# Attention and a gated MLP on one core: which PSUM banks the joined attention-times-V blocks sum into

## The chip, the cores and the metric

The kernel runs on 1 core of one Trainium2 chip. The metric is the time of one execution on the device in microseconds; the time shown for a kernel is the median of its runs. The engines are TensorE (matmul; in the profile PE, its weight loads PEld), VectorE (DVE), ScalarE (ACT), GpSimd (POOL) and SyncE (SP, which here only issues DMAs).

## The reference

One transformer layer in parallel form: the same normalized input goes through sliding-window attention (A) and through a gated MLP (B), and both are added to the input.

```python
S, D, H, Dh, W, F = 2048, 576, 32, 18, 256, 4608      # bf16 inputs, batch 1
def _A_ref(x, wqkv, wo):
    q, k, v = ...                                     # x @ wqkv, split in 32 heads of 18
    scores = jnp.einsum("bhqd,bhkd->bhqk", q, k) * (Dh ** -0.5)
    mask = (idx[:, None] - idx[None, :] >= 0) & (idx[:, None] - idx[None, :] < W)
    p = _softmax(jnp.where(mask[None, None], scores, -1e9), axis=-1)
    o = jnp.einsum("bhqk,bhkd->bhqd", p, v)
    return o.transpose(0, 2, 1, 3).reshape(B, S, D) @ wo
def _B_ref(x, w1, w3, w2):
    h = _silu(x @ w1) * (x @ w3)
    return h @ w2
xn = _layernorm(x)
return x + _A_ref(xn, A_wqkv, A_wo) + _B_ref(xn, B_w1, B_w3, B_w2)
```

## The kernel before

**Order of work.** `add` (from L55) records every operation with the tiles that it reads and writes; `resolve` works out the semaphores that each needs, and each engine then runs its own operations in the order of recording. So the order in the file is the order on each engine, and a tile that is still being read or written by another engine becomes a wait.

The 2048 rows are worked on in NC = 4 chunks of 512 rows. A chunk has three stages:

- Projections of Q, K and V (`proj_begin`, `proj_part`, L502), in chunks 1 to 3; those of chunk 0 come ahead of the loop.
- The W1/W3 stage: 36 units, `for u in range(NF)`. A unit makes 128 of the 4608 columns of h. `unit_pairs` (L767) is called for nine steps n = 0 to 8, each a matmul of 64 rows of the array for W3 and one for W1, side by side, into two banks of 512 columns. Then `unit_tanh` (L776, ScalarE) reads the W1 bank, and `unit_h` issues two products on VectorE: `gs` (L782, from the tanh and the W1 bank) and `hT` (L785, from `gs` and the W3 bank). When the second has ended, both banks are free.
- The W2 stage: `p2_list` makes a list of items and `p2_item` issues them (`p2_mm`, L838). Output rows go in four groups of 128 (`tt`), in two halves of 288 columns, so there are four accumulators in each half, kept in `ACC[half]`. Items `w2` are steps over h, items `wo` and `wr` steps over the attention's output in `oT`; `wr` is what is left over of it. `q` is a pair of accumulators: q = 0 is `ACC[half][0:2]`, q = 1 is `ACC[half][2:4]`. In `rest()` there is one `wr` item for each pair; in half 0 both come first, ahead of the nine W2 tiles (`fc`) of sixteen `w2` items each. Items other than those for the whole 128 rows are two matmuls of 64 rows of the array.

**Attention inside the W1/W3 stage.** `score_step` puts one step of scores between matmul steps of a unit: `scores` (L632) writes the two scores' banks `SC`, `exps` (L641, ScalarE) reads them and writes probabilities into a slot, `masks` (L669, POOL) multiplies the slot by the mask. Slots lie in `pt`, and in memory lent by others: `stage`, `hT`, from unit 30 `uq`, `ofin` and `od`, from unit 32 a weight buffer (shown as `w`). Heads are in eight groups; two groups make a pair j = 0 to 3, whose attention-times-V (`pv`, L697) sums into two banks. `BLOCKS` says which pairs are done together: in chunk 0 pairs 0 and 1 alone and (2, 3) joined; in chunks 1 to 3 (0, 1) and (2, 3). A joined block is issued by `pv_block(u, True)` in the middle of a unit, at the (u, n) of `AT`: block (0, 1) at (16, 2), (16, 3) and (16, 5) in chunks 1, 2 and 3, block (2, 3) at (35, 1), (35, 3), (35, 4) and (35, 5) in chunks 0 to 3. `HOLD` = 10 keeps scores steps away in the ten matmul steps before it, and `nxt, soon` keep them away for 17 steps after.

**PSUM.** Of the eight banks two are `SC`, the other six are three pairs in a ring:

```python
        JOBS, SC = ((0, 1), (2, 3), (4, 5)), (6, 7)
        def job():
            nonlocal job_ctr
            i = job_ctr % 3
            job_ctr += 1
            return JOBS[i]
```

Every unit and every projection takes the next pair. In the loop over units, `b0 = jobs[u] = job()` comes ahead of the unit's steps, so a block in the middle of unit u takes what follows unit u's pair. `ACC` for the W2 stage consists of the pairs of units 34 and 35, the ring pair of the last block, and `SC`.

**Output of a block.** `pv_out` (L714, VectorE) transposes one bank into a float32 tile: the first into `uq`, the second into the memory of `ofin`, the third and fourth into two `pt` slots that `borrow` lends. `o_recip` (L718, VectorE) takes the reciprocals of the sums, `o_scale` (L723, POOL) scales one group into `oq`, `o_turn` (L730, VectorE, two halves) turns it back into `od`, and `o_pack` (L755) sends a pair from `od` to `oT` by DMA from SP. `later(u, what)` puts work off to just after `unit_h(u)`; what is put off beyond unit 35 is issued after the sixth item of the W2 stage.

Of the kernel before, what the change touches and what calls it, by code (L numbers as in the profile page):

```python
# [44 lines left out]
class _Prog:  # L45
# [13 lines left out]
    def add(self, eng, fn, r=(), w=(), j=(), dma=None, after=()):  # L59
        deps = []  # L60
        for k in r:
            deps += self.bufs[k].writers
        for k in w:
            g = self.bufs.get(k)
            if g is not None:
                deps += g.ahead(eng)
        for k in j:
            g = self.bufs[k].before
            if g is not None:
                deps += g.ahead(eng)  # L70
        op = _Op(eng, fn, deps + list(after), dma)
        op.after = tuple(after)
        self.n[eng] += 1
        op.pos = self.n[eng]
        if dma is not None:
            self.dma_count[dma] = self.dma_count.get(dma, 0) + 16
            op.cnt = self.dma_count[dma]
        for k in r:
            self.bufs[k].readers.append(op)
        for k in w:  # L80
            self.bufs[k] = _Gen([op], self.bufs.get(k))
        for k in j:
            self.bufs[k].writers.append(op)
        for k in w:
            if self.bufs[k].before is not None:
                self.bufs[k].before.before = None
        self.ops.append(op)
        return op
# [76 lines left out]
def bass_parallel_sum__sliding_block__glu_gated_swiglu__prompt_kernel(  # L165
# [21 lines left out]
    NF = F // 128  # L187
# [3 lines left out]
    scale = float(Dh) ** -0.5  # L191
# [6 lines left out]
    with ExitStack() as es:  # L198
# [80 lines left out]
        JOBS, SC = ((0, 1), (2, 3), (4, 5)), (6, 7)  # L279
        ACC = [[], []]  # L280
        job_ctr = 2
# [6 lines that stand above are left out]
# [418 lines left out]
        def borrow(slots):  # L706

            for i, n in enumerate(slots):
                uqs[2 + i:3 + i] = [pt[:, n, :, :].rearrange("p r q -> p (r q)").bitcast(dt.float32)]
                uq_keys[2 + i:3 + i] = [[("pt", n)]]  # L710

        def pv_out(b, i):
            to = uqs[i]
            add("dve", lambda e: e.transpose(to, PS[:, b, :]), r=[("ps", b)], w=uq_keys[i])  # L714

        def o_recip(i):
            u3 = uqs[i].rearrange("p (n d) -> p n d", d=32)
            add("dve", lambda e: e.reciprocal(rden[i][:], u3[:, :, Dh]), r=uq_keys[i], w=[("rden", i)])  # L718

        def o_scale(i):  # L720
            u3 = uqs[i].rearrange("p (n d) -> p n d", d=32)
            o3 = oq[:, :].rearrange("p (n d) -> p n d", d=32)[:, :, 0:Dh]
            add("pool", lambda e: e.tensor_tensor(  # L723
                o3, u3[:, :, 0:Dh], rden[i][:].unsqueeze(2).to_broadcast([128, CH // 32, Dh]), ALU.mult),
                r=uq_keys[i] + [("rden", i), "oq0"], w=["oq"])

        def o_turn(g, half):
            i = g // 2 % NOD
            c0 = half * (CH // 2)
            add("dve", lambda e: e.transpose(od[i][:, g % 2, c0:c0 + CH // 2], oq[:, c0:c0 + CH // 2]),  # L730
                r=["oq", "oq0"], **{"j" if half or g % 2 else "w": [("od", i)]})
# [58 lines left out]
        def p2_list(c):  # L790

            seq = []
            for half in range(2):
                sw = half

                def phases(items):
                    nonlocal sw
                    for turn in (sw, 1 - sw):
                        for q in range(2):
                            yield from ((q, turn, it) for it in items)  # L800
                    sw = 1 - sw

                def rest():
                    return [("wr", half, 0, q, 0, 0) for q in range(2)]

                whole = half == 1 and c + 1 == NC
                if half == 0:
                    seq += rest()
                for fc in range(NFC - whole):
                    tile = [("w2", half, fl, q, turn, fc) for q, turn, fl in phases(range(4))]  # L810
                    seq += tile + [("next", half, 0, 0, 0, fc)]
                if whole:
                    seq.append(("keep", half, 0, TB - 1, 0, 0))
                    for tt in range(TB):
                        for turn in (None,) if tt < TB - 1 else (-2, -1):
                            seq += [("w2", half, fl, tt, turn, NFC - 1) for fl in range(4)]
                            seq += [("wo", half, kd, tt, turn, 0) for kd in range(5)]
                            seq += [("out", half, 0, tt, turn, 0)]
                    continue
                seq += [("wo", half, kd, q, turn, 0) for q, turn, kd in phases(range(2))]  # L820
                two = [("wo", half, kd, q, turn, 0) for q, turn, kd in phases(range(2, 4))]
                ends = rest() if half == 1 else []
                seq += two[:4]
                for q in range(2):
                    seq += two[4 + 2 * q:6 + 2 * q] + (ends[q:q + 1] if half == 1 else [])
                    seq += [("out", half, 0, 2 * q + r, 0, 0) for r in range(2)]
            return seq
# [210 lines left out]
        main, rest = span_main, span_last  # L1038
# [5 lines left out]
        for c in range(NC):  # L1044
# [23 lines left out]
            jobs = {}  # L1068
# [3 lines left out]
            def later(u, what):  # L1072
                side.setdefault(u, []).append(what)
# [29 lines left out]
            def pv_block(u, mid=False):  # L1103
                nonlocal next_pv, clock, free, job_ctr, nxt, soon
                block = BLOCKS[c][next_pv]
                assert u > turned.get(c, -1) + 1, (c, u, turned)
                next_pv += 1
                ends = next_pv == len(BLOCKS[c])
                pairs = [job(), SC] if ends else [job() for _ in block]
                for j, banks in zip(block, pairs):  # L1110
                    pv(c, j, banks)
                clock += PV_COST[c] * len(block)
                if len(block) == 2:
                    nxt, soon = max(nxt, clock + 17), max(soon, clock + 17)
                groups = range(2 * block[0], 2 * block[-1] + 2)
                was = [pt_of[(c, g, s)] for g in groups for s in range(NS)]
                assert all(NF - 2 * NHP + 2 * n > u for kind, n in was if kind == "h"), (c, u)
                was = [sl for sl in was if sl[0] != "h"]
                lent = [n for kind, n in was if kind == "pt"][-2:] if len(block) == 2 else []
                free += [sl for sl in was if sl not in [("pt", n) for n in lent]] + [("pt", n) for n in lent]  # L1120

                def drain(pairs=pairs, lent=lent):
                    borrow(lent)
                    for i in range(2 * len(pairs)):
                        pv_out(pairs[i // 2][i % 2], i)
                    for i in range(2 * len(pairs)):
                        o_recip(i)
                    o_scale(0)

                drain() if mid else later(u, drain)  # L1130
                if ends:
                    job_ctr -= 1
                    ACC[:] = [[*jobs[NF - 2], *pairs[0]], [*SC, *jobs[NF - 1]]]
                else:
                    job_ctr += mid
                k = 0
                for i, g in enumerate(groups):
                    for half in range(2):
                        k += 1 if (i, half) not in ((0, 1), (2, 1)) else 0
                        later(u + k, lambda g=g, half=half: o_turn(g, half))  # L1140
                    if i + 1 < len(groups):
                        later(u + k, lambda i=i: o_scale(i + 1))
                turned[c] = u + k
                for i, j in enumerate(block):
                    later(u + (4 + 3 * i if len(block) == 2 else 5), lambda j=j: o_pack(j, "sp"))
                    for n in range(4, 12, 2 if c else 1) if j == 0 else ():
                        later(u + n // 2 + 3 if c else u + n + 1,
                              lambda n=n: o_pack(0, "sp", n, n + 2) if c else o_pack(0, "act", n, n + 1))
# [19 lines left out]
            for u in range(NF):  # L1168
# [50 lines left out]
                if c == 0 and u == 18:  # L1219
                    rows = A_wo[0:4 * Dh, :].rearrange("(n d) f -> n d f", d=Dh)  # L1220
                    add("sp", lambda e: e.dma_start(wo[126:128, 0:4, :], rows[:, 0:2, :].rearrange("n d f -> d n f")),
                        j=["wo"], dma="wo")
                    for p in range(2):
                        add("sp", lambda e, p=p: e.dma_start(wo[64 * p:64 * p + 64, 4, :], rows[:, 2:Dh, :]),
                            j=["wo"], dma="wo")
# [11 lines left out]
            banks = ()  # L1237
# [52 lines left out]
```

## Time and profile before

| | us |
|---|---|
| median of 3 runs | 558.56 (558.46 to 558.62) |
| the profiled execution | 558.54 |
| its span in the trace | 556.8 |
| mean granted TensorE clock | 1.00 |

The lines of the profile stand in the prediction. Groups read: line, engine, operation, out<-in by tile names, shapes, count | busy us, mean ns of one | idle time of the engine just before them, and what ended it. Lines of the timeline read: start (us), duration (us), engine, line, operation, out<-in, how many were merged [idle before, and what ended it]. A duration of several merged matmuls runs from the start of the first to the end of the last; ends of matmuls are modelled. Lines of the list of waits read: who waited <- for whom: total us, how often, the longest. Chunk 0's W1/W3 stage ends near 101 us of the span, those of chunks 1, 2 and 3 near 239, 377 and 514 us; each time the W2 stage follows for some 40 us.

### The profile page before, as it was taken

How to read it: one execution, taken by the hardware profiler on the slowest of the kernel's cores; microseconds unless marked ns; L12 is line 12 of the kernel's file. 1: busy time of each engine (PE TensorE's matmuls, PEld its weight loads, DVE VectorE, ACT ScalarE, POOL GpSimd, SP SyncE). 2: the span in 40 equal slices, each digit the busy share in tenths (PEclk: the TensorE clock that was granted, in tenths of full speed). 3: DMA queues.
4: the chain of work that ended last, by engine and by line, in shares of the span. 5: the costliest groups of instructions: out<-in, count | busy, mean ns of one | idle time of the engine just before them, and what ended most of it. 6: DMA issues, size and time to landing. Idle time of an engine off the chain costs nothing.

```text
span 556.8 us, 18354 instructions
## 1 busy us (share of the span) xinstructions
PE 551.2 (99%) x8071; PEld 365.6 (66%) x8071; DVE 313.2 (56%) x587; ACT 259.3 (47%) x365; POOL 211.2 (38%) x380
## 2 busy tenths in 40 slices
PE   8999999999999999999999999999999999999998
PEld 5555544777688644477768854557887665445787
DVE  8466797710478886651057978655105567866311
ACT  7457776000387568600047757760005774875000
POOL 4424675400056565530005755643000553663100
PEclk9999999999999999999999999999999999999999
DMA  9997899587567853756646985476673673641750
GB/s 249 204 199 174 197 209 213 133 201 184 134 141 165 164 136 102 171 144 193 186 106 139 177 151 137 106 167 162 176 184 87 138 171 101 151 116 44 192 152 23
DMA packets 128038, 86.00 MB, mean 154 GB/s; under 512 B 35702, under 2 KB 125646, under 8 KB 127958
## 3 DMA queue, kind: packets, MB, share of 16 engines
q1 hardware_dynamic: 89138, 62.80, 50.3%
q10 hardware_dynamic: 38820, 22.02, 15.7%
q8 instruction: 63, 1.03, 0.8%
q14 instruction: 17, 0.14, 0.1%
HBM read 71.29 MB, written 2.36 MB: 132 GB/s over the span
## 4 chain that ended last, share of the span: by engine, by line
PE 96%; DVE 1%; ACT 1%; issue 1%; DMA 0%; ACTq 0%
PE ps L767 50%; PE ps L838 29%; PE ps L502 9%; PE ps L632 5%; PE ps L697 3%; DMA xp<-in_A_x_dram 0%; DVE gs L782 0%; DVE hT L785 0%; ACT th L776 0%; ACTq L567 0%; ACT stage L515 0%; DVE stats L398 0%; ACT hT L392 0%; DVE uq L714 0%; PE ps L431 0%
## 5 line engine op out<-in xcount | busy, mean ns | idle before, releaser
L767 PE MATMUL ps<-xnT,w 64*128 64x512 bf16 x1400 | 190.1, 376 | 0.0
L767 PE MATMUL ps<-xnS,w 64*128 64x512 bf16 x1120 | 156.9, 376 | 0.0
L838 PE MATMUL ps<-w,hT 64*128 64x288 bf16 x2292 | 143.5, 282 | 0.0
L782 DVE SCALAR_TENSOR_TENSOR gs<-th,ps 128x512 bf16<-128x512 bf16 x144 | 97.9, 680 | 79.7 <-ACT th L776 79.1
L838 PEld LDWEIGHTS ps<-w,hT 64*128 64x128 bf16 x2292 | 115.3, 94 | 26.0 <-issue 0.2
L767 PEld LDWEIGHTS ps<-xnT,w 64*128 64x128 bf16 x1400 | 80.3, 94 | 52.8 <-issue 0.6
L776 ACT ACTIVATE th<-ps 128x512 bf16<-128x512 f32 x144 | 85.6, 594 | 61.3 <-PE ps L767 60.1
L785 DVE SCALAR_TENSOR_TENSOR hT<-gs,ps 128x512 bf16<-128x512 bf16 x144 | 98.9, 687 | 5.0
L669 POOL TENSOR_TENSOR pt<-pt,mk 128x256 bf16<-128x256 bf16 (+1 forms) x143 | 85.7, 625 | 26.7 <-ACT pt L641 26.7
L641 ACT ACTIVATE pt<-ps 128x1024 bf16<-128x1024 f32 (+1 forms) x80 | 80.8, 1010 | 27.0 <-PE ps L632 26.5
L767 PEld LDWEIGHTS ps<-xnS,w 64*128 64x128 bf16 x1120 | 64.2, 94 | 42.9 <-issue 0.6
L669 POOL TENSOR_TENSOR hT<-hT,mk 128x256 bf16<-128x256 bf16 (+1 forms) x52 | 30.4, 605 | 161.5 <-ACT hT L641 161.5
L515 ACT ACTIVATE stage<-ps 128x512 bf16<-128x512 f32 x16 | 9.6, 597 | 139.6 <-PE ps L502 137.3
L869 DVE TENSOR_TENSOR ofin<-ps,xp 128x288 bf16<-128x288 f32 x31 | 12.2, 451 | 99.2 <-PE ps L838 99.2
L632 PE MATMUL ps<-qv,kv 64*128 64x320 bf16 (+4 forms) x528 | 56.0, 260 | 0.0
L632 PEld LDWEIGHTS ps<-qv,kv 64*128 64x128 bf16 x528 | 30.3, 94 | 23.9 <-ACT uq L641 1.1
L502 PE MATMUL ps<-xnT,wp 64*128 64x512 bf16 (+1 forms) x360 | 39.3, 355 | 0.0
L730 DVE STREAM_TRANSPOSE od<-oq 128x256 bf16<-128x256 bf16 x64 | 25.4, 425 | 12.2 <-POOL oq L723 12.2
L641 ACT ACTIVATE hT<-ps 128x1024 bf16<-128x1024 f32 (+1 forms) x28 | 28.4, 1015 | 7.8 <-PE ps L632 7.6
L669 POOL TENSOR_TENSOR stage<-stage,mk 128x256 bf16<-128x256 bf16 (+1 forms) x44 | 24.9, 587 | 12.6 <-ACT stage L641 12.6
L502 PEld LDWEIGHTS ps<-xnT,wp 64*128 64x128 bf16 x360 | 21.4, 94 | 12.0 <-ACT va L551 0.2
L641 ACT ACTIVATE stage<-ps 128x1024 bf16<-128x1024 f32 (+1 forms) x24 | 24.3, 1014 | 6.1 <-PE ps L632 6.0
(92 smaller groups left out, 403.6 us busy)
## 6 DMA issues: line engine op xcount, KB each, us to landing
w<-in_B_w_dram SPq DMA_DIRECT2D x210, 192.0 KB, 4.2
w<-in_B_w_dram ACTq DMA_DIRECT2D x70, 288.0 KB, 3.5
xp<-in_A_x_dram SPq DMA_DIRECT2D x29, 144.0 KB, 4.2
out_dram<-ofin SPq DMA_DIRECT2D x31, 72.0 KB, 1.7
xnS<-xnT SPq DMA_DIRECT2D x8, 256.0 KB, 4.7
oT<-od SPq DMA_DIRECT2D x56, 36.0 KB
pt<-in_A_wqkv_dram SPq DMA_DIRECT2D x4, 288.0 KB, 5.4
hT<-in_B_w_dram SPq DMA_DIRECT2D x6, 192.0 KB, 7.3
```

Source lines behind the costliest of these rows:

```text
L502: op = add("pe", lambda e, out_=out_, st=st, mv=mv, n=n, r0=r0, first=first: e.matmul(out_, st, mv, start=first, stop=(part == 1 and n == ...
L632: add("pe", lambda e, r0=r0, out_=out_, kb=kb, q0=q0, nb=nb: e.matmul(out_, kb4[r0:r0 + 64, g, kb + NV - NB, :] if kb < 0 else kv[r0:r0 + ...
L641: add("act", lambda e: e.activation(pt_slot(sl)[:, :, 0:w], PS[:, SC[0]:SC[1] + 1, 0:w], ACT.Exp, scale=scale), r=[("ps", b) for b in SC], ...
L669: add("pool", lambda e, vb=vb, mm=mm: e.tensor_tensor(vb, vb, mm, ALU.mult), r=(key if n == 0 else []) + ["mk"], **{"w" if n == 0 else "j" ...
L697: add("pe", lambda e, p=p, q=q, pr=pr, sl=sl, g=g, pos=pos, q0=q0, nb=nb, col=col, first=first, n=n: e.matmul(PS[32 * q:32 * q + VW, banks ...
L730: add("dve", lambda e: e.transpose(od[i][:, g % 2, c0:c0 + CH // 2], oq[:, c0:c0 + CH // 2]), r=["oq", "oq0"], **{"j" if half or g % 2 els ...
L767: op = add("pe", lambda e, n=n, r0=r0, r=r, k=k, src=src: e.matmul(PS[:, b0 + r, :], wt[r0:r0 + 64, k, fl * 128:(fl + 1) * 128], src, star ...
L776: add("act", lambda e: e.activation(th[i][:], PS[:, bg, :], ACT.Tanh, scale=0.5), r=[("ps", bg)], w=[("th", i)])
L782: add("dve", lambda e: e.scalar_tensor_tensor(out=gs[i][:], in0=th[i][:], scalar=1.0, in1=PS[:, bg, :], op0=ALU.add, op1=ALU.mult), r=[("t ...
L785: add("dve", lambda e: e.scalar_tensor_tensor(out=hT[:, u, :], in0=gs[i][:], scalar=0.5, in1=PS[:, bu, :], op0=ALU.mult, op1=ALU.mult), r= ...
L838: op = add("pe", lambda e: e.matmul(PS[:, bank, 0:w], stat, move, start=new, stop=False, skip_group_check=True, **tile), r=keys, after=hel ...
L869: add("dve", lambda e: e.tensor_tensor(ofin[:, o, :], PS[:, bank, 0:HD], xp[xs[n]][:, d0:d0 + HD], ALU.add), r=[("ps", bank), ("xp", xs[n] ...
```

## The change

Five things are changed in two functions:

1. In a joined block the first pair of heads sums into `SC`, and the second into the ring's next pair, in every such block. Before, block (0, 1) took two ring pairs, and block (2, 3) one ring pair for pair 2 and `SC` for pair 3.
2. Block (0, 1) no longer advances the ring by one extra place (`job_ctr += mid` is gone).
3. Where block (2, 3) is drained, the ring pair, now that of pair 3, is still transposed first: the order of pairs is turned round there (`order`), and with it the order of scaling, turning and packing.
4. In block (0, 1) of chunks 1 to 3 only the first two transposes are issued at once; the other two, the reciprocals and the first scaling come after the products of the unit that the block stands in.
5. In half 0 of the W2 stage, four `w2` items of the first pair of accumulators come between the two `wr` items.

```diff
@@ p2_list
-                if half == 0:
-                    seq += rest()
                 for fc in range(NFC - whole):
                     tile = [("w2", half, fl, q, turn, fc) for q, turn, fl in phases(range(4))]
+                    if fc == half == 0:
+                        tile = [*rest()[:1], *tile[:4], *rest()[1:], *tile[4:]]
                     seq += tile + [("next", half, 0, 0, 0, fc)]
@@ pv_block
-                pairs = [job(), SC] if ends else [job() for _ in block]
+                pairs = [SC, job()] if len(block) == 2 else [job()]
                 for j, banks in zip(block, pairs):
                     pv(c, j, banks)
...
-                groups = range(2 * block[0], 2 * block[-1] + 2)
+                order = list(zip(block, pairs))[::-1 if ends else 1]
+                groups = [2 * j + i for j, _ in order for i in range(2)]
+                banks = [b for _, two in order for b in two]
...
-                def drain(pairs=pairs, lent=lent):
+                def drain(part=range(len(banks))):
                     borrow(lent)
-                    for i in range(2 * len(pairs)):
-                        pv_out(pairs[i // 2][i % 2], i)
-                    for i in range(2 * len(pairs)):
+                    for i in part:
+                        pv_out(banks[i], i)
+
+                def scale():
+                    for i in range(len(banks)):
                         o_recip(i)
                     o_scale(0)
 
-                drain() if mid else later(u, drain)
                 if ends:
+                    drain()
+                    scale()
                     job_ctr -= 1
-                    ACC[:] = [[*jobs[NF - 2], *pairs[0]], [*SC, *jobs[NF - 1]]]
+                    ACC[:] = [[*jobs[NF - 2], *pairs[1]], [*SC, *jobs[NF - 1]]]
+                elif mid:
+                    drain(range(2))
+                    later(u, lambda: drain(range(2, 4)))
+                    later(u, scale)
                 else:
-                    job_ctr += mid
+                    later(u, drain)
+                    later(u, scale)
...
-                for i, j in enumerate(block):
+                for i, (j, _) in enumerate(order):
                     later(u + (4 + 3 * i if len(block) == 2 else 5), lambda j=j: o_pack(j, "sp"))
```

## The prediction

> **What bounds the kernel now.** I read the page first, then the list of waits, then the timeline around the seven joined attention-times-V blocks and the starts of the W2 stage. The page and the waits:
>
> ```profile
> PE 551.2 (99%) x8071; PEld 365.6 (66%) x8071; DVE 313.2 (56%) x587; ACT 259.3 (47%) x365; POOL 211.2 (38%) x380
> PE 96%; DVE 1%; ACT 1%; issue 1%; DMA 0%; ACTq 0%
> PE ps L697 <- DVE hT L785: 1.0, 4, 0.3
> PEld ps L838 <- DVE ofin L714: 0.6, 2, 0.4
> DVE od L730 <- POOL oq L723: 12.2, 12, 1.9
> ```
>
> TensorE is busy for 99% of the span and holds 96% of the chain that ended last. No matmul is added or removed, so the change can only shorten or lengthen TensorE's waits. The waits name two places that it touches: the joined blocks (L697), held by the products of an earlier unit (L785), and the W2 stage (L838), held by the transposes (L714). An idle figure of modelled matmuls hides part of a stall, so I price each by the distance between matmul starts, against the same place where nothing is waited for.
>
> **The block at unit 16.** Old order: pair j = 0 takes the ring's next banks (those of unit 14), pair 1 the ones after (those of unit 15). Chunks 1, 2 and 3, in this order:
>
> ```profile
> 189.70 0.81 PE L767 MATMUL ps<-xnT,w 64*128 64x512 bf16 x6
> 190.02 0.69 DVE L785 SCALAR_TENSOR_TENSOR hT<-gs,ps 128x512 bf16<-128x512 bf16 x1
> 190.76 0.31 PE L697 MATMUL ps<-hT,va 64*20 64x320 bf16 x4 [0.24 <-DVE hT L785]
> 191.48 0.69 DVE L785 SCALAR_TENSOR_TENSOR hT<-gs,ps 128x512 bf16<-128x512 bf16 x1
> 191.78 0.30 PE L697 MATMUL ps<-hT,va 64*20 64x192 bf16 x8
> 192.31 0.31 PE L697 MATMUL ps<-pt,va 64*20 64x320 bf16 x4 [0.23 <-DVE hT L785]
> 327.86 1.04 PE L767 MATMUL ps<-xnT,w 64*128 64x512 bf16 x8
> 329.14 0.31 PE L697 MATMUL ps<-hT,va 64*20 64x320 bf16 x4 [0.24 <-DVE hT L785]
> 330.16 0.30 PE L697 MATMUL ps<-hT,va 64*20 64x192 bf16 x8
> 330.55 0.31 PE L697 MATMUL ps<-pt,va 64*20 64x320 bf16 x4
> 466.50 0.38 PE L767 MATMUL ps<-xnS,w 64*128 64x512 bf16 x2
> 466.81 0.31 PE L697 MATMUL ps<-hT,va 64*20 64x320 bf16 x4
> 467.82 0.30 PE L697 MATMUL ps<-hT,va 64*20 64x192 bf16 x8
> 468.02 0.31 PE L697 MATMUL ps<-pt,va 64*20 64x320 bf16 x4
> ```
>
> Two matmuls make a step; 0.216 us separate steps (row 194.86 below: five in 1.24 us, the last of them lasting 0.376). Chunk 3 waits for nothing: 0.31 us from the unit's last step to the block, 0.20 from the last wave of pair 0 to pair 1. In chunk 1 the last step starts at 189.70 + 2 x 0.216 = 190.13, the block at 190.76, 0.05 after the product of 190.02 ends: 0.63, so 0.32 too much. Pair 1 starts 0.53 after 191.78, 0.14 after the product of 191.48 ends: 0.33 too much. Chunk 2: 328.51 to 329.14 is 0.63 (0.32 too much), 330.16 to 330.55 is 0.39 (0.19 too much). Chunk 3 has nothing to give.
>
> With the change pair 0 goes to the scores' banks. Their last scores were written at least ten steps before (HOLD; 2.16 us), which leaves the exponentials time to read them out. Pair 1 takes unit 14's banks, free when the old pair 0 started. All four delays go: **0.32 + 0.33 + 0.32 + 0.19 = 1.16 us**. At worst none goes, if the scores' banks were busy as long.
>
> **What the changed ring costs.** The old code skipped one place after the block; now it doesn't. Counting on: unit 17 takes unit 15's pair (free before the block ended), unit 18 the pair of unit 16, unit 19 that of pair 1. Unit 18 has only unit 17's nine steps behind which unit 16's tanh and two products can pass. No scores step fills in: the next is due 17 steps after the block, in unit 18. Chunk 1:
>
> ```profile
> 193.66 1.31 DVE L714 STREAM_TRANSPOSE pt<-ps 128x512 f32<-128x512 f32 x2 [0.24 <-PE ps L697]
> 194.86 1.24 PE L767 MATMUL ps<-xnT,w 64*128 64x512 bf16 x10
> 195.15 0.30 DVE L718 RECIPROCAL rden<-pt 128x16 f32<-128x16 f32 x2
> 195.28 0.60 ACT L776 ACTIVATE th<-ps 128x512 bf16<-128x512 f32 x1 [4.56 <-PE ps L767]
> 195.91 0.69 DVE L782 SCALAR_TENSOR_TENSOR gs<-th,ps 128x512 bf16<-128x512 bf16 x1 [0.46 <-ACT th L776]
> 196.63 0.69 DVE L785 SCALAR_TENSOR_TENSOR hT<-gs,ps 128x512 bf16<-128x512 bf16 x1
> 196.80 0.59 PE L767 MATMUL ps<-xnT,w 64*128 64x512 bf16 x4
> ```
>
> The row of 194.86 begins with unit 16's last step, that of 196.80 with unit 17's. Unit 18 would start at 196.80 + 0.216 = 197.02. Unit 16's second product ends at 196.63 + 0.69 = 197.32; TensorE restarts after a single DVE signal in 0.06 (row 514.42 below, behind a transpose that ends at 514.36). So 197.38: **0.36 us late**. The distance is the same wherever the block stands in unit 16, since all of it lies after that unit's last step, so three chunks cost **1.08 us**; no row shows this wait itself. Behind the waiting matmul stands all of TensorE (unit 18, its scores step), and behind those ScalarE's tanh and exponential, so the whole stage moves by that much. Bounds: 0 if the pair is free after all, 3 x 0.44 = 1.32 with the slowest restart above (0.14). I take 0.06, the nearest in kind, since no tiling changes there.
>
> A rule of the Trainium skill speaks against this part: Perfetto Trace Analysis, section Optimizing Tensor Performance, Matmuls, asks that independent groups rotate through PSUM banks so that the evacuation of one overlaps the next group's matmuls. By that rule the old skip kept two units before a reuse and the new ring keeps one; taken alone that is rival E. The trace agrees as far as 2.46 us of evacuation (194.86 to 197.32) outlast 2.16 us of steps, but it has waits on the other side too.
>
> **VectorE's order.** Transposes 2 and 3 (1.31 us, row 193.66), four reciprocals (to 195.45, 0.48) and the first scaling move behind unit 16's products. Queued behind them are unit 17's products: chain free at 197.32 + 1.79 = 199.11, unit 17's products end at 200.52. Unit 20 needs them, at 197.38 + 2 x 1.94 = 201.26 at the earliest (scores steps push it on). Unit 19 needs transpose 3, at 198.6, and starts no sooner than 199.3. Both covered: cost 0. Without that cover each microsecond of lag beyond 0.7 costs one.
>
> **The block at unit 35.** Old: pair 2 on unit 33's banks, pair 3 on the scores' banks. Chunks 1, 2, 3:
>
> ```profile
> 234.26 1.03 PE L767 MATMUL ps<-xnT,w 64*128 64x512 bf16 x8
> 235.62 0.52 PE L697 MATMUL ps<-pt,va 64*20 64x320 bf16 x31 [0.33 <-DVE hT L785]
> 372.29 1.24 PE L767 MATMUL ps<-xnT,w 64*128 64x512 bf16 x10
> 373.65 0.52 PE L697 MATMUL ps<-pt,va 64*20 64x320 bf16 x31
> 510.41 0.38 PE L767 MATMUL ps<-xnS,w 64*128 64x512 bf16 x2
> 510.72 0.52 PE L697 MATMUL ps<-pt,va 64*20 64x320 bf16 x32
> ```
>
> Last step to block: 235.62 - 234.91 = 0.71, 373.65 - 373.15 = 0.50, 0.31. The third is the undisturbed figure again, so 0.40 and 0.19 are waits for unit 33, and go when pair 2 starts in the scores' banks: **0.59 us**. Chunk 0's block I leave at 0, which errs against the change if it waits at all.
>
> **The start of W2.** The banks of the block's ring pair receive the second `wr` group, after transposes 0 and 1. Chunks 1, 2, 3:
>
> ```profile
> 239.43 39.69 PE ps L838 x648
> 239.27 0.41 PE L838 MATMUL ps<-wo,oT 64*128 64x288 bf16 x4
> 377.08 0.57 PE L838 MATMUL ps<-wo,oT 64*128 64x288 bf16 x4
> 513.05 0.72 DVE L714 STREAM_TRANSPOSE uq<-ps 128x512 f32<-128x512 f32 x1 [1.19 <-PE ps L697]
> 513.69 0.67 DVE L714 STREAM_TRANSPOSE ofin<-ps 128x512 f32<-128x512 f32 x1
> 513.93 0.78 PE L838 MATMUL ps<-wo,oT 64*128 64x288 bf16 x4
> 514.42 0.09 PEld L838 LDWEIGHTS ps<-wo,oT 64*128 64x128 bf16 x1 [0.39 <-DVE ofin L714]
> ```
>
> Four matmuls take 0.41 us undisturbed; 0.16 and 0.37 more are waits. Now the ring pair is summed last, but the first transpose already started only when the whole block had ended (513.05): its target `uq` held probabilities of pair 3. So it moves by nothing. Four W2 steps go ahead of the second `wr`, each of two matmuls and so of 39.69 us / 648 x 2 = 0.12 us (first row, a piece of the chain of waits), 0.49 together, more than 0.37. They use unit 34's banks and products, ready long before. Gain: **0.53 us**; if the steps found something of their own to wait for, 0. The pack DMAs of pairs 3 and 2 change places on SP; the flush comes after the same six items, and the output projection that reads them runs nine W2 tiles (over 17 us) later: 0.
>
> **Sum.** 1.16 + 0.59 + 0.53 - 1.08 = 1.20 us saved. The profiled execution took 558.54 us (span 556.8); 558.54 - 1.20 = 557.34, and the median of the runs is 558.56, so **557.35 us**, 0.22% faster. What a measurement here can tell from no change is about 0.2%, 1.12 us: the forecast lies just past that line, at 557.44.
>
> **Rivals.**
>
> *B, the new wait takes most of it.* Unit 18 stalls longer than the rows say, 0.44 plus one refill of about 0.2 us (the distance between pairs in chunk 3), 0.64 x 3 = 1.92: 558.54 - 2.28 + 1.92 = **558.2**. For it: no row shows that wait. Against: the same restart in W2 took 0.06 and the old waits were priced in whole starts. Or the W2 gain fails: 557.9.
>
> *C, VectorE's lag becomes the bound (slower).* The place is the turn of the scaled output (L730), which stands in VectorE's queue between unit 17's and unit 18's products and waits for POOL's scaling, itself in line with the masks:
>
> ```profile
> L730 DVE STREAM_TRANSPOSE od<-oq 128x256 bf16<-128x256 bf16 x64 | 25.4, 425 | 12.2 <-POOL oq L723 12.2
> ```
>
> After two turns of this mean (0.85 us) unit 18's products run from 201.4 to 202.8; unit 21 wants the banks at 197.38 + 3 x 1.94 = 203.2. Beyond 0.4 us of waiting there, all goes to TensorE. The longest such wait listed is 1.9 us: 3 x 1.5 = 4.5, 557.35 + 4.5 = **561.9**. Against: the scaling needs only the first reciprocal, and unit 17's products give it 1.4 us.
>
> *D, unit 18's pair is free (the ring isn't what I counted).* Then 558.54 - 2.28 = **556.3**. Against: the deleted skip.
>
> *E, the old delays stay and only the new wait counts (slower).* If the 0.63 and 0.5 us at the blocks are the price of starting a block and not of waiting, only the lost distance between units is left: 558.54 + 1.08 = **559.6**. Against: the undisturbed 0.31 and 0.20 of chunk 3. The rule of the Trainium skill quoted above (Perfetto Trace Analysis, Matmuls) would give this case.
>
> **Chances.** Forecast 0.65, with its own range 557.0 to 557.8, of which 0.45 lies below 557.44; B 0.18; C 0.07; D 0.07; E 0.03. Faster 0.45 + 0.07 = 0.52, same 0.20 + 0.18 = 0.38, slower 0.07 + 0.03 = 0.10. The range 556.9 to 558.3 holds the forecast and B, and leaves out C, D and E.
>
> **What would show it.** In the profile after: no wait of L697 on L785 at the blocks of chunks 1 to 3, 0.31 us from last step to block and 0.20 between pairs; a new wait of L767 on L785 at the start of unit 18 three times, 0.2 to 0.3 us of modelled idle; no wait of L838 on L714. Wrong: a longer or second stall in units 18 to 21, a wait of the block for the exponentials, or a W2 start that waits for `hT` or `w`.

## The result, and the profile after

| | before | changed |
|---|---|---|
| median, us | 558.62 (558.44 to 560.62, 11 runs) | 557.11 (556.89 to 558.14, 11 runs) |
| ratio of the times | | 0.9971, 95% interval 0.9962 to 0.9981 |
| the profiled execution, us | 558.54 | 558.14 |
| its span, us | 556.8 | 556.4 |
| start of the long piece of W1/W3 matmuls in chunk 0 (120 in the chain of waits) | 21.04 | 22.11 |
| from there to the end of the span | 535.76 | 534.29 |

The change saves 1.51 us, 0.29% with an interval of 0.19% to 0.38%. The forecast was 557.35 us and 0.22%.

The profiled execution of the changed kernel is the slowest of its eleven: one of its first loads of x came about a microsecond later (the third statistics row on VectorE, L398, waits 1.20 us for it and starts at 6.80 us instead of 5.74), which moves everything behind it. That belongs to this execution and not to the program: in e9 below, the same program again, the long piece starts at 21.05. So below I compare traces from the start of chunk 0's W1/W3 matmuls on (the last row, here called the body). By the body the change saves 1.47 us, close to the medians.

The page and the list of waits after:

```profile
PE 551.5 (99%) x8071; PEld 362.1 (65%) x8071; DVE 312.6 (56%) x587; ACT 259.6 (47%) x365; POOL 211.2 (38%) x380
PE 98%; DVE 1%; ACT 1%; issue 0%
DVE od L730 <- POOL oq L723: 12.2, 12, 1.9
PEld ps L767 <- DVE hT L785: 1.7, 3, 0.7
PE ps L767 <- DVE hT L785: 0.4, 2, 0.2
```

The waits of the joined blocks (L697) on unit products (L785) and of W2 (L838) on transposes (L714) are gone from the list. In their place the units (L767) wait for the products of an earlier unit, three times. VectorE's wait for POOL's scaling (L730) is what it was, to the digit.

The block at unit 16, timeline of the changed kernel, chunks 1, 2 and 3:

```profile
190.72 0.81 PE L767 MATMUL ps<-xnT,w 64*128 64x512 bf16 x6
191.46 0.31 PE L697 MATMUL ps<-hT,va 64*20 64x320 bf16 x4
192.48 0.30 PE L697 MATMUL ps<-hT,va 64*20 64x192 bf16 x8
192.56 0.32 PE L697 MATMUL ps<-pt,va 64*20 64x320 bf16 x4
328.05 1.04 PE L767 MATMUL ps<-xnT,w 64*128 64x512 bf16 x8
329.02 0.31 PE L697 MATMUL ps<-hT,va 64*20 64x320 bf16 x4
330.04 0.30 PE L697 MATMUL ps<-hT,va 64*20 64x192 bf16 x8
330.22 0.31 PE L697 MATMUL ps<-pt,va 64*20 64x320 bf16 x4
466.20 0.38 PE L767 MATMUL ps<-xnS,w 64*128 64x512 bf16 x2
466.51 0.31 PE L697 MATMUL ps<-hT,va 64*20 64x320 bf16 x4
467.53 0.30 PE L697 MATMUL ps<-hT,va 64*20 64x192 bf16 x8
467.62 0.32 PE L697 MATMUL ps<-pt,va 64*20 64x320 bf16 x4
```

From the unit's last step to the block it is now 0.31 us (191.46 - 191.15), 0.32 and 0.31; before, 0.63, 0.63 and 0.31. From the last wave of the first pair to the second pair it is 0.08, 0.18 and 0.09; before, 0.53, 0.39 and 0.20. The block lost 1.40 us of waiting.

Two units further on, chunks 1, 2 and 3. Each first row begins with unit 16's last step, the second is its second product; the third holds the first matmuls of unit 18 (in chunk 1 behind unit 17's last step):

```profile
195.11 1.24 PE L767 MATMUL ps<-xnT,w 64*128 64x512 bf16 x10
196.88 0.69 DVE L785 SCALAR_TENSOR_TENSOR hT<-gs,ps 128x512 bf16<-128x512 bf16 x1
197.22 0.79 PE L767 MATMUL ps<-xnT,w 64*128 64x512 bf16 x4
332.55 1.24 PE L767 MATMUL ps<-xnT,w 64*128 64x512 bf16 x10
334.32 0.69 DVE L785 SCALAR_TENSOR_TENSOR hT<-gs,ps 128x512 bf16<-128x512 bf16 x1
335.07 0.61 PE L767 MATMUL ps<-xnT,w 64*128 64x512 bf16 x4 [0.20 <-DVE hT L785]
469.52 1.24 PE L767 MATMUL ps<-xnT,w 64*128 64x512 bf16 x10
471.29 0.69 DVE L785 SCALAR_TENSOR_TENSOR hT<-gs,ps 128x512 bf16<-128x512 bf16 x1
472.04 1.04 PE L767 MATMUL ps<-xnT,w 64*128 64x512 bf16 x8 [0.20 <-DVE hT L785]
```

Without a wait unit 18 starts ten steps of 0.216 us after unit 16's last: 334.71 in chunk 2, 471.68 in chunk 3. It starts at 335.07 and 472.04, 0.06 us after the product's end: 0.36 us late each time. In chunk 1 the two steps of the third row are 0.79 - 0.38 = 0.41 apart, so unit 18 starts at 197.63 instead of 197.27. Together 1.08 us. The listed 0.20 of idle is only the part that shows between modelled matmul ends.

The block at unit 35 in chunks 1 and 2, then the start of W2 in chunk 3:

```profile
234.88 1.03 PE L767 MATMUL ps<-xnT,w 64*128 64x512 bf16 x8
235.84 0.52 PE L697 MATMUL ps<-pt,va 64*20 64x320 bf16 x32
372.33 1.24 PE L767 MATMUL ps<-xnT,w 64*128 64x512 bf16 x10
373.50 0.52 PE L697 MATMUL ps<-pt,va 64*20 64x320 bf16 x32
513.03 0.82 PE L767 MATMUL ps<-xnS,w 64*128 64x512 bf16 x6
513.13 0.72 DVE L714 STREAM_TRANSPOSE uq<-ps 128x512 f32<-128x512 f32 x1 [1.30 <-PE ps L697]
513.77 0.67 DVE L714 STREAM_TRANSPOSE ofin<-ps 128x512 f32<-128x512 f32 x1
514.02 0.65 PE L838 MATMUL ps<-w,hT 64*128 64x288 bf16 x8
514.51 0.29 PE L838 MATMUL ps<-wo,oT 64*128 64x288 bf16 x2
```

The blocks start 0.31 us after the last step (235.84 - 235.53, 373.50 - 373.19); before, 0.71 and 0.50. In W2 the second `wr` item starts at 514.51, right behind the four `w2` items (514.02 + 4 x 0.1225). The second transpose ends at 514.44, 0.07 us before. That is hardly more than the 0.06 us that TensorE took to restart behind such a transpose in the kernel before, so it only just makes it. Before, the first transpose began with the next unit step (513.05 against 513.06); now it begins 0.10 us after it.

### The profile page after: what moved, and what is told of

It reads as the page before. It is cut to its first block, busy times and chain, and to the rows that moved or that the text cites. A ratio compares the mean times of both kernels' runs of the same rounds, so it can differ in the third digit from the quotient of the medians.

```text
span 556.4 us, 18354 instructions
## 1 busy us (share of the span) xinstructions
PE 551.5 (99%) x8071; PEld 362.1 (65%) x8071; DVE 312.6 (56%) x587; ACT 259.6 (47%) x365; POOL 211.2 (38%) x380
## 4 chain that ended last, share of the span: by engine, by line
PE 98%; DVE 1%; ACT 1%; issue 0%
PE ps L767 50%; PE ps L838 29%; PE ps L502 9%; PE ps L632 5%; PE ps L697 3%; PE ps L908 1%; DVE gs L782 0%; DVE hT L785 0%; ACT th L776 0%; ACT xnT L444 0%; PE ps L431 0%; DVE xn L416 0%; ACT xnT L450 0%; DVE stats L398 0%; ACT sd L371 0%
## 5 line engine op out<-in xcount | busy, mean ns | idle before, releaser
L767 PE MATMUL ps<-xnT,w 64*128 64x512 bf16 x1400 | 190.6, 376 | 0.4 <-DVE hT L785 0.4
L767 PE MATMUL ps<-xnS,w 64*128 64x512 bf16 x1120 | 156.9, 376 | 0.0
L838 PE MATMUL ps<-w,hT 64*128 64x288 bf16 x2292 | 143.7, 282 | 0.0
L838 PEld LDWEIGHTS ps<-w,hT 64*128 64x128 bf16 x2292 | 112.3, 94 | 29.4 <-issue 0.2
L767 PEld LDWEIGHTS ps<-xnT,w 64*128 64x128 bf16 x1400 | 80.2, 94 | 54.2 <-DVE hT L785 1.7
L785 DVE SCALAR_TENSOR_TENSOR hT<-gs,ps 128x512 bf16<-128x512 bf16 x144 | 98.9, 687 | 4.9
L767 PEld LDWEIGHTS ps<-xnS,w 64*128 64x128 bf16 x1120 | 64.3, 94 | 42.8 <-issue 0.6
L869 DVE TENSOR_TENSOR ofin<-ps,xp 128x288 bf16<-128x288 f32 x31 | 12.2, 451 | 98.3 <-PE ps L838 98.3
L730 DVE STREAM_TRANSPOSE od<-oq 128x256 bf16<-128x256 bf16 x64 | 25.4, 426 | 12.2 <-POOL oq L723 12.2
```

Of the source, the lines that this page charges most:

```text
L767: op = add("pe", lambda e, n=n, r0=r0, r=r, k=k, src=src: e.matmul(PS[:, b0 + r, :], wt[r0:r0 + 64, k, fl * 128:(fl + 1) * 128], src, star ...
L785: add("dve", lambda e: e.scalar_tensor_tensor(out=hT[:, u, :], in0=gs[i][:], scalar=0.5, in1=PS[:, bu, :], op0=ALU.mult, op1=ALU.mult), r= ...
L838: op = add("pe", lambda e: e.matmul(PS[:, bank, 0:w], stat, move, start=new, stop=False, skip_group_check=True, **tile), r=keys, after=hel ...
L869: add("dve", lambda e: e.tensor_tensor(ofin[:, o, :], PS[:, bank, 0:HD], xp[xs[n]][:, d0:d0 + HD], ALU.add), r=[("ps", bank), ("xp", xs[n] ...
```

## The experiments

All kernels compute the whole reference. "Body" is the span from the start of chunk 0's long W1/W3 piece, in the one profiled execution; medians of different rows come partly from different chips. Spans are read to 0.1 us, so a difference of two bodies is good to about 0.1 us, and it holds the scatter of single executions too. The intervals of e1 to e4 overlap that of the changed kernel: their medians alone don't tell them from it, and what I say of them rests on the rows of their traces.

| kernel | median, us | ratio to before, 95% interval | body, us |
|---|---|---|---|
| before | 558.6 | | 535.76 |
| changed | 557.11 | 0.9971, 0.9962 to 0.9981 | 534.29 |
| e1: changed, old W2 order | 557.93 | 0.9980, 0.9965 to 0.9996 | 535.26 |
| e2: changed, old block (0, 1) | 557.47 | 0.9973, 0.9963 to 0.9983 | 534.61 |
| e3: changed, old block (2, 3) | 557.75 | 0.9978, 0.9968 to 0.9987 | 534.86 |
| e4: changed, drained at once | 557.49 | 0.9972, 0.9961 to 0.9982 | 534.49 |
| e5: ring places exchanged | 556.00 | 0.9961, 0.9947 to 0.9975 | 533.17 |
| e6: e5 with late transposes | 560.80 | 1.0045, 1.0029 to 1.0061 | 538.06 |
| e7: before, only the W2 order | 558.02 | 0.9992, 0.9983 to 1.0001 | 535.27 |
| e8: before, only block (2, 3) | 558.25 | 0.9994, 0.9985 to 1.0003 | 535.38 |
| e9: changed, again | 557.15 | 0.9972, 0.9960 to 0.9983 | 534.25 |
| e10: as e5, beside e9 | 556.04 | 0.9958, 0.9946 to 0.9971 | 534.89 |

The profiled execution of e10 holds a stall of TensorE that no other trace has (0.8 us of idle with no releaser), so its body isn't used.

### e1: the old order of W2's first steps

```diff
+                if half == 0:
+                    seq += rest()
                 for fc in range(NFC - whole):
                     tile = [("w2", half, fl, q, turn, fc) for q, turn, fl in phases(range(4))]
-                    if fc == half == 0:
-                        tile = [*rest()[:1], *tile[:4], *rest()[1:], *tile[4:]]
```

> The changed kernel with the old order of W2's first steps (both wr items first). Bank theory: the second wr group waits again for the ring pair's second transpose, 0.16 us in chunk 2 and 0.37 us in chunk 3, so 557.11 + 0.53 = 557.6 us, with a wait of L838 on L714 in the list. Rival (the stall only moved to another place of the W2 stage, so the new order gives nothing): 557.1 us, no such wait.

Timeline of e1 at the start of W2 in chunk 2, and in chunk 3:

```profile
376.33 0.68 PE L838 MATMUL ps<-wo,oT 64*128 64x288 bf16 x4
376.71 0.09 PEld L838 LDWEIGHTS ps<-wo,oT 64*128 64x128 bf16 x1 [0.28 <-DVE ofin L714]
...
513.56 0.40 PE L838 MATMUL ps<-wo,oT 64*128 64x288 bf16 x3
514.15 0.09 PEld L838 LDWEIGHTS ps<-wo,oT 64*128 64x128 bf16 x1 [0.50 <-DVE ofin L714]
```

The wait is back, and larger than before the change: 0.68 - 0.41 = 0.27 us in chunk 2; in chunk 3 the load of the last weights waits 0.50 (before: 0.39). That is the extra 0.1 us seen above: the ring pair is summed last now, and its first transpose waits for the block's very last matmul. The body is 0.97 us longer. Of this some 0.3 us have nothing to do with the edit: from the start of the body to chunk 0's W2 stage e1 takes 80.72 us, the changed kernel 80.48, and from there to chunk 1's W2 stage 137.14 against 137.06, though the two programs differ there only in the order at the start of chunk 0's W2 stage, which takes 39.69 us in both. That much single traces scatter.

### e2: the old block (0, 1)

```diff
-                pairs = [SC, job()] if len(block) == 2 else [job()]
+                pairs = [SC, job()] if ends else [job() for _ in block]
...
                 elif mid:
-                    drain(range(2))
-                    later(u, lambda: drain(range(2, 4)))
-                    later(u, scale)
+                    drain()
+                    scale()
+                    job_ctr += 1
```

> The changed kernel with block (0, 1) as before: two ring pairs, the ring skips a place, all four transposes at once. Bank theory: the waits of L697 come back (1.16 us) and the wait at unit 18 goes (1.08 us), so 557.11 + 0.08 = 557.2 us; the block's move by itself is worth next to nothing. Rival 1 (the new wait is the dearer one): under 556.8 us. Rival 2 (this block brought the gain): 558 us or more.

Body +0.32 us against the changed kernel: more than the 0.08 expected, still a small part of the whole. Three waits in this block were traded for three waits two units later. That it is 0.32 and not 0.08 is the distance between the pairs, which fell in the changed kernel below the 0.20 us that I had taken as undisturbed (0.08 and 0.09 in chunks 1 and 3); in e2 it is 0.53, 0.39 and 0.20 again.

### e3: the old block (2, 3)

```diff
-                pairs = [SC, job()] if len(block) == 2 else [job()]
+                pairs = ([job(), SC] if ends else [SC, job()]) if len(block) == 2 else [job()]
...
-                order = list(zip(block, pairs))[::-1 if ends else 1]
+                order = list(zip(block, pairs))
...
-                    ACC[:] = [[*jobs[NF - 2], *pairs[1]], [*SC, *jobs[NF - 1]]]
+                    ACC[:] = [[*jobs[NF - 2], *pairs[0]], [*SC, *jobs[NF - 1]]]
```

> The changed kernel with block (2, 3) as before: pair 2 on the ring's banks, pair 3 on the scores' banks, drained in the old order. Bank theory: the start of the block waits for unit 33 again, 0.40 us in chunk 1 and 0.19 in chunk 2, so 557.11 + 0.59 = 557.7 us, with starts 0.71 and 0.50 us after the unit's last step. Rival (the distance is the price of starting a block): 557.1 us.

Timeline of e3, chunk 1, then chunk 2:

```profile
234.06 1.03 PE L767 MATMUL ps<-xnT,w 64*128 64x512 bf16 x8
234.59 0.69 DVE L785 SCALAR_TENSOR_TENSOR hT<-gs,ps 128x512 bf16<-128x512 bf16 x1
235.42 0.52 PE L697 MATMUL ps<-pt,va 64*20 64x320 bf16 x31 [0.33 <-DVE hT L785]
371.90 1.24 PE L767 MATMUL ps<-xnT,w 64*128 64x512 bf16 x10
373.26 0.52 PE L697 MATMUL ps<-pt,va 64*20 64x320 bf16 x31
```

235.42 - 234.71 = 0.71 and 373.26 - 372.76 = 0.50, the old distances to the digit; body +0.57 us. The distance was a wait and not the price of starting a block.

### e4: drained at once

```diff
                 elif mid:
-                    drain(range(2))
-                    later(u, lambda: drain(range(2, 4)))
-                    later(u, scale)
+                    drain()
+                    scale()
```

> The changed kernel, but block (0, 1) is drained and its reciprocals are taken all at once, ahead of unit 16's products; banks and ring as changed. Bank theory: unit 18 waits for unit 16's second product, so what delays that product counts in full. Four transposes and four reciprocals end 0.4 us after the tanh in chunk 3 and about 0.05 us after it in chunks 1 and 2, so 557.11 + 0.5 = 557.6 us. Rival (the order on VectorE is off the path): 557.1 us.

A miss in size. Timeline of e4 in chunk 3: unit 16's last step (first row), its tanh, the last reciprocals, its first product, unit 18:

```profile
468.51 1.24 PE L767 MATMUL ps<-xnT,w 64*128 64x512 bf16 x10
468.93 0.60 ACT L776 ACTIVATE th<-ps 128x512 bf16<-128x512 f32 x1 [3.80 <-PE ps L767]
469.53 0.31 DVE L718 RECIPROCAL rden<-pt 128x16 f32<-128x16 f32 x2
469.75 0.63 DVE L782 SCALAR_TENSOR_TENSOR gs<-th,ps 128x512 bf16<-128x512 bf16 x1
471.15 1.04 PE L767 MATMUL ps<-xnT,w 64*128 64x512 bf16 x8 [0.33 <-DVE hT L785]
```

The product begins 0.2 us after the tanh, not 0.4, and unit 18 starts at 471.15 instead of 470.67: 0.48 us late against 0.36. I had added the durations of VectorE's rows end to end, while successive rows overlap. In chunks 1 and 2 unit 18 is late by 0.35 and 0.36 us, as in the changed kernel. So the split drain saves some 0.12 us in one chunk and nothing in the others. The body is 0.20 us longer, but 0.17 of that arises before chunk 0's W2 stage (80.65 us against 80.48), where the programs are the same; the ratio is as good as unchanged. The sign is the theory's: what delays the second product counts. The split drain is worth hardly anything.

### e5 and e10: two places of the ring exchanged

Unit 18 is made to reuse the second pair's banks, which are transposed early, and unit 19 those of unit 16.

```diff
-        JOBS, SC = ((0, 1), (2, 3), (4, 5)), (6, 7)
+        JOBS, SC = [(0, 1), (2, 3), (4, 5)], (6, 7)
...
-                pairs = [SC, job()] if len(block) == 2 else [job()]
+                if len(block) == 2 and not ends:
+                    a, b = job_ctr % 3, (job_ctr + 1) % 3
+                    JOBS[a], JOBS[b] = JOBS[b], JOBS[a]
+                    pairs = [SC, JOBS[b]]
+                else:
+                    pairs = [SC, job()] if ends and len(block) == 2 else [job()]
...
-                    drain(range(2))
-                    later(u, lambda: drain(range(2, 4)))
-                    later(u, scale)
+                    drain()
+                    scale()
```

> The changed kernel, but two places of the ring are exchanged at block (0, 1): unit 17 on unit 15's pair as now, unit 18 on pair 1's banks, unit 19 on unit 16's; all four transposes at once, so that pair 1's banks are free by then. Bank theory: transposes 2 and 3 end about 2 us ahead of unit 18, and unit 16's products pass behind units 17 and 18, so the wait at unit 18 goes without another in its place: 557.11 - 1.08 = 556.0 us. Rival (VectorE's backlog is what holds unit 18, or the wait moves on to units 19 to 21): 557.1 us.

> The kernel with the exchanged ring again, beside the changed kernel on the same chip. Bank theory: 1.1 us less than the changed kernel, 556.0 us. Rival (the first pair of numbers came from different chips): within 0.3 us of it.

> The changed kernel again, on the same chip as the next one, for a direct comparison: 557.1 us.

Timeline of e5 in chunk 1: transposes 2 and 3, unit 16's last step (first of the second row), its second product, then unit 17's last step with unit 18's first:

```profile
193.26 1.27 DVE L714 STREAM_TRANSPOSE pt<-ps 128x512 f32<-128x512 f32 x2
194.14 1.24 PE L767 MATMUL ps<-xnT,w 64*128 64x512 bf16 x10
195.92 0.69 DVE L785 SCALAR_TENSOR_TENSOR hT<-gs,ps 128x512 bf16<-128x512 bf16 x1
196.09 0.59 PE L767 MATMUL ps<-xnT,w 64*128 64x512 bf16 x4
```

Unit 18's first step follows unit 17's last by 0.59 - 0.38 = 0.21 us, so it starts at 196.30, while unit 16's product runs on until 196.61. The banks that it needs were free from 194.53. The list of waits of e5 has no wait of L697, L767 or L838 on VectorE left. It takes 556.0 us, and on one chip 556.04 against 557.15 for the changed kernel: 1.1 us less, as priced, and 2.55 us less than before on that chip. Four of e10's five runs (555.97 to 556.30) lie below every run of e9 (557.00 to 557.25). This version beats both.

### e6: the exchanged ring with late transposes

The `JOBS` and `pairs` edit of e5, with the changed kernel's split drain left in.

> The exchanged ring, but with transposes 2 and 3 behind unit 16's products as in the changed kernel. Bank theory: now unit 18 waits for the fourth transpose, which ends 1.3 us after unit 16's second product: 0.36 + 1.25 = 1.6 us in each of three chunks, so 556.0 + 4.8 = 560.8 us. Rival (unit 18's wait doesn't hang on the banks): as without this, 556 to 557.1 us.

Timeline of e6, chunk 1:

```profile
194.17 1.24 PE L767 MATMUL ps<-xnT,w 64*128 64x512 bf16 x10
196.55 1.31 DVE L714 STREAM_TRANSPOSE pt<-ps 128x512 f32<-128x512 f32 x2
197.32 0.39 PE L767 MATMUL ps<-xnT,w 64*128 64x512 bf16 x1 [0.82 <-DVE pt L714]
197.91 0.39 PE L767 MATMUL ps<-xnT,w 64*128 64x512 bf16 x1 [0.21 <-DVE pt L714]
```

Unit 18's first matmul waits for transpose 2, its second (the other bank) for transpose 3, which ends at 197.86. Due at 194.17 + 2.16 = 196.33, it goes on at 197.91: 1.58 us late, where 1.6 was expected. 560.8 us, 4.8 us over e5. So it is the bank that unit 18 reuses that sets its start, and one line of order on VectorE turns the best of these kernels into the worst.

### e7 and e8: one part alone, on the kernel before

e7 is the kernel before with the `p2_list` part of the change. e8 is e2 with the old `p2_list`, so that only block (2, 3) differs from before.

> The kernel before with only the new order of W2's first steps. Bank theory: the waits of 0.16 and 0.37 us in chunks 2 and 3 go, nothing else changes: 0.53 us less than before, about 558.1 us, and no wait of L838 on L714. Rival (this order only helps together with the new banks): no change.

> The kernel before with only block (2, 3) changed (banks and order of draining). Bank theory: the block no longer waits for unit 33, 0.59 us less; but the ring pair is now summed last, so its first transpose waits for the block's very last matmul, and with the old order of W2's first steps that costs about 0.1 us in each of chunks 2 and 3: 0.4 us less than before, about 558.2 us. Rival (without the new W2 order the gain is given back whole there): no change.

Bodies: -0.49 us (0.53 expected) and -0.38 us (0.4 expected); the medians, 558.02 and 558.25 against 558.59, agree, though each ratio's interval reaches just past 1, so the medians alone don't show either gain. In e8 the wait of W2 stands in the list with 0.8 us instead of 0.6, and its W2 stage is 0.05 us longer in chunk 1 (39.74 against 39.69) and 0.10 in chunk 2 (39.95 against 39.85). Together (e2 against before) the two parts give 1.15 us, some 0.3 more than the sum of each alone: the bank change by itself lengthens the wait that the new W2 order hides.

## Why the prediction was right

It named the waits that go, the one that comes, and their prices. Step by step, in us:

| step | forecast | measured in the trace after |
|---|---|---|
| block (0, 1): waits that go | -1.16 | -1.40 |
| unit 18: the wait that comes | +1.08 | +1.08 |
| block (2, 3): waits that go | -0.59 | -0.59, and -0.05 in chunk 0 |
| second `wr` item: waits that go | -0.53 | -0.53 |
| VectorE's order | 0 | 0 |
| sum | -1.20 | -1.49 |

The sum on the right agrees with the body's 1.47 and the medians' 1.51.

- The term that was mis-sized is "0.20 from the last wave of pair 0 to pair 1". I took it for a floor because the trace names no wait beside it in chunk 3. In the changed kernel it is 0.08, 0.18 and 0.09, which gives the 0.24 us by which the first row is off. "Chunk 3 waits for nothing" was wrong for this distance, as a row of the kernel before shows:

```profile
467.19 0.69 DVE L785 SCALAR_TENSOR_TENSOR hT<-gs,ps 128x512 bf16<-128x512 bf16 x1
```

  This is unit 15's second product, and the old pair 1 took unit 15's banks. It ends at 467.88, and pair 1 starts at 468.02, 0.14 us later: the same 0.14 as in chunk 1 (192.17 to 192.31), where the wait is named. In all three chunks of before, e2, e7 and e8, which have the old block, pair 1 starts 0.14 or 0.15 us after that product. So chunk 3 waited too, by about 0.12 us, and with the other banks this wait is gone. The 0.18 of chunk 2 is no feature of chunk 2: in e9, the same program, the distances are 0.15, 0.08 and 0.08, and in e5 and e10, one program with this block, 0.18, 0.08, 0.09 and 0.08, 0.08, 0.09. What now and then adds 0.1 us there stays open.
- Unit 18's wait came as counted from the ring, with 0.06 us of restart: rival B (a longer stall) and D (no stall) are out. e5 and e6 show that it hangs on the bank: with another bank it is gone, or 1.58 us. The rule of the Trainium skill that I held against the change (Perfetto Trace Analysis, Optimizing Tensor Performance, Matmuls: groups should rotate through PSUM banks so that evacuation overlaps) is borne out as far as that wait; e5 adds that with as many banks it is their order that decides.
- Rival C (VectorE's lag): the wait for POOL's scaling is unchanged at 12.2 us in 12 places, and units 19 to 21 don't wait. The cover that I named held.
- Rival E (the distance is the price of a block) fell with e3, and in the trace after: every joined block now starts 0.31 to 0.33 us after the unit's last step. That remainder fits a rule of the Trainium skill, that changing the tiling mode drains TensorE (TensorEngine Tiling (Array Packing), Key Properties); no run here took the switch away, so its share is not shown.
- "So it moves by nothing", said of the first transpose at unit 35, was wrong by 0.1 us: its target `uq` was free at the same time, but its source bank is now the one written last. It cost nothing, because the four `w2` items still cover it. That was luck: they take 0.49 us, the old wait of chunk 3 was 0.37, and with the 0.1 us it would have been some 0.47. e1 and e8, which lack them, pay for it.

## What to carry to other kernels

When a ring of PSUM banks gets a guest, count for each later user how much matmul time lies between the last reader's start and the reuse, and compare it with the whole evacuation (here 2.46 us against 2.16). If it is too short for one place, exchange two places before adding work or buffers: the bank that was read earliest should be reused first.

Price a wait by the distance between matmul starts, against a place with the same neighbours that doesn't wait; the idle figure beside a modelled matmul showed 0.20 of 0.36 us. And before calling a distance a floor, look for a row that ends just ahead of it: the 0.20 us of chunk 3 showed no idle figure, and was in part a wait.

## What the runs showed that I had not expected

- Two matmuls that run side by side wait for their banks one by one: in e6 the first of unit 18 starts at 197.32 and its partner at 197.91.
- VectorE's rows overlap: in e4 the first product starts at 469.75, before the reciprocals end at 469.53 + 0.31 = 469.84. Adding durations put the end of a queue 0.2 us too late.
- Single executions of one program differ by a microsecond at the start (22.11 and, in e9, 21.05 us to the long piece of the changed kernel), and different programs by 0.1 to 0.3 us within stretches that are the same in both. A change of a quarter of a per cent had to be read from the body, or from the median of some ten runs.
